# Row numbers for the sparse expert slots: one-hot matmuls on chip in place of scatters to memory

## The chip, the cores and the metric

One Trainium2 chip, one of its cores. The metric is the device time of one execution in microseconds (us). Engines: PE (TensorE), DVE (VectorE), ACT (ScalarE), POOL (GpSimd), SP (SyncE, which here only issues DMAs).

## The reference

Three layers follow one another: a decaying linear attention (2 batches, 8 heads, 768 positions, 64 wide), a sparse mixture of experts, and a dense one.

```python
def reference(**kwargs):
    ...
    attn_out = _attn_ref(**attn_kwargs)
    x = np.ascontiguousarray(attn_out.transpose(0, 2, 1, 3)).reshape(B * S, H * D)   # 1536 rows of 512
    x = _moe_ref(x=x, **moe_kwargs)
    return _moe2_ref(x=x, **moe2_kwargs)

def _moe_ref(x, modality_id, w_gate, modality_bias, w1, w2):
    logits = x @ w_gate + modality_bias[modality_id]
    e_idx = np.argmax(logits, axis=1)                 # one of 8 experts for each row
    ...
    for e in range(E):
        mask = e_idx == e
        h = np.maximum(x[mask] @ w1[e], 0.0)
        out[mask] = gate_w[mask, None] * (h @ w2[e])

def _moe2_ref(x, w_gate, w1, w2):
    logits = x @ w_gate
    P = np.exp(logits - logits.max())
    for _ in range(8):
        ...                                           # rows and columns of P scaled in turn
    for e in range(E):
        out += P[:, e:e + 1] * (np.maximum(x @ w1[e], 0.0) @ w2[e])
```

## The kernel before

**Attention and routing** (`attention_and_routing`, lines 360 to 561). The 1536 tokens are M = 12 blocks of C = 128. A loop over t (line 510) interleaves, in one written order for all engines, the scores of block t, the outputs of block t-1, the gate scores of block t-2 (`rows`), and, for pairs of blocks, `gates` (the expert of each token, a one-hot `oh`), `weighted` (the rows scaled and stored to the DRAM table `xs`, a DMA on ACT's queue) and `place`. `place` (lines 182 to 199) counts with bf16 matmuls how many earlier tokens went to the same expert: `posf` is N times the expert's number plus the token's rank in that expert, and `posi` the same as an integer.

**Lists of rows.** `scatter_id` (lines 201 to 205) writes, for one block, 128 row numbers of 4 bytes each into the DRAM table `treg` at the places `posi`, by an indirect DMA on POOL's queue. 12 such scatters stand in the loop; `treg` is cleared by one DMA at the start (line 407). Whoever wants the rows of a slot reads 384 consecutive numbers of `treg` back into `gidx` (`gather_ids`, line 340, from a start that POOL loads into a register), and then gathers the rows of `xs` with three indirect DMAs (`gather_rows`, line 344).

**Sparse experts.** Tokens of an expert are worked on in slots of 272. One slot is early: after 6 blocks `early_table` (line 212) picks the fullest expert, SP starts to load its weights, and at t = 11 its rows are gathered and transposed (`xprep`, line 352). `early_slot` (line 587) computes it right after the attention and prepares slot 0. Then come at least NREST = 5 further slots (`rest_slot`, `slot`, lines 627 to 658); in this run exactly 5, called slots 0 to 4 below. A slot has steps f = 0 to 8: at f the first matmul group of piece f (`mm1`, 12 matmuls of 272 columns, evicted as `hb` by ACT and DVE), the second one of piece f-2 (`second_of`), the splitting of the next weights into two parts on ACT and DVE (`conv1`, `conv2`, by `split`, lines 297 to 306), which SP reloads behind it. At f = 0 it issues the gather of the next slot's rows and the read of the row numbers of the slot after that; at f = 4 and 5 it transposes the gathered rows.

**Compact positions.** Slots leave their results in `x2T` in the order of experts. The dense layer works in that order, and needs for each compact position the token it belongs to (`tokmap`), to scatter the output rows (line 849). `compact_ranks`, `compact_starts` and `compact_positions` compute the position of each token in slot 1; 12 further scatters (`compact_scatters`, 6 in slot 1 and 6 in slot 2) write the token numbers to the DRAM table `tokd`, and one DMA reads it back (line 972).

**Dense experts.** From about 277 us to the end; the change leaves its code as it is but for that one DMA.

The order on every engine is the order in which the program is written (`tc.manual_schedule()`). An engine that waits holds up all that is written behind it on that engine. The lines that the change is about:

```python
            inst = G.indirect_dma_start(out=treg, out_offset=bass.IndirectOffsetOnAxis(ap=posi[:, m:m + 1], axis=0), in_=seqi[:, m:m + 1], in_offset=None).ins
...
            G.dma_start(out=gidx[z], in_=treg[ds(pos, 384)].rearrange("(z p) o -> p (z o)", p=128))
...
                inst = G.indirect_dma_start(out=tokd, out_offset=bass.IndirectOffsetOnAxis(ap=posi[:, m:m + 1], axis=0), in_=toki[:, m:m + 1], in_offset=None).ins
```

## Time and profile before

| | |
|---|---|
| median of 3 runs | 1321.52 us (1318.6 to 1322.06) |
| the profiled execution | 1313.04 us, of which 1311.4 us are the span from its first to its last instruction |
| busy in the span | PE 96%, DVE 51%, ACT 38%, POOL 35% |
| mean granted TensorE clock | 0.985 of full speed |
| DMA | 117.76 MB, 61735 packets, 8376 of them under 512 B |

The profile names each instruction by line, engine, operation and tiles (written <- read). "Idle before" is the time for which the engine did nothing just before an instruction; the name behind "<-" is what ended that wait. PEclk is the clock that TensorE was granted (1.00 is 2.4 GHz, 0.50 is 1.2 GHz), DMA the busy share of the core's 16 DMA engines.

### The profile page before, as it was taken

The page shows a single profiled execution, that of the slowest core. Times are in us where ns is not written, and L with a number is a line of the kernel's source. Part 1 is how long each engine was busy: PE and PEld are TensorE (multiplying, and loading weights), DVE is VectorE, ACT ScalarE, POOL GpSimd, SP SyncE. Part 2 cuts the span into 40 slices and gives each one's busy share as a digit, 9 for nine tenths or more (in the row PEclk, how much of TensorE's full clock was granted, in tenths as well). Part 3 has the DMA queues.
Part 4 walks back from the last instruction along what each step waited for, and adds up shares of the span by engine and source line. Part 5 has one row for each costly group of instructions (what it writes and reads, how often), then busy time and mean ns, then how long its engine had stood idle before and what let it go on. Part 6 is the DMA issues. An engine that isn't in the chain of part 4 may idle for free.

```text
span 1311.4 us, 19165 instructions
## 1 busy us (share of the span) xinstructions
PE 1254.2 (96%) x7164; PEld 1141.5 (87%) x7164; DVE 664.6 (51%) x1248; ACT 498.4 (38%) x996; POOL 457.8 (35%) x464
## 2 busy tenths in 40 slices
PE   5868998989999999999999999999999999999997
PEld 4758997988999999999998999999999999999996
DVE  5546655646454545445454546354535454545453
ACT  1225545531234334333434342233433343434341
POOL 3532152014433333333333336333333333333332
PEclk9989998989999999999999999999999999999999
DMA  8887697530022222222222222222222222222201
GB/s 289 142 192 154 195 151 192 184 115 1 18 72 73 73 64 65 64 73 63 67 65 73 66 88 91 62 81 65 65 70 68 65 64 65 73 65 75 71 25 48
DMA packets 61735, 117.76 MB, mean 90 GB/s; under 512 B 8376, under 2 KB 10048, under 8 KB 61632
## 3 DMA queue, kind: packets, MB, share of 16 engines
q1 hardware_dynamic: 55744, 105.67, 29.1%
q0 software_dynamic: 3408, 7.14, 2.0%
q10 hardware_dynamic: 2480, 3.64, 1.2%
q8 instruction: 58, 0.95, 0.3%
q14 instruction: 45, 0.37, 0.1%
HBM read 110.05 MB, written 6.37 MB: 89 GB/s over the span
## 4 chain that ended last, share of the span: by engine, by line
PE 77%; DVE 1%; POOL 0%; issue 0%; POOLq 0%
PE banks L868 13%; PE banks L867 13%; PE banks L866 13%; PE banks L831 12%; PE banks L832 12%; PE banks L833 12%; PE banks L704 0%; POOL out_dram L849 0%; PE banks L710 0%; PE banks L736 0%; DVE Pm L730 0%; DVE Pm L740 0%; DVE tab L728 0%; POOLq L1004 0%; DVE tab L738 0%
## 5 line engine op out<-in xcount | busy, mean ns | idle before, releaser
L820 POOL TENSOR_TENSOR w1r<-sraw,w1r 128x1024 fp32r<-128x1024 f32 x56 | 134.6, 2403 | 573.1 <-ACT w1r L819 573.1
L868 PE MATMUL banks<-w2r,hb 128*128 128x512 f32 x750 | 294.7, 393 | 0.0
L867 PE MATMUL banks<-w2r,hb 128*128 128x512 f32 x750 | 294.1, 392 | 0.0
L866 PE MATMUL banks<-w2r,hb 128*128 128x512 f32 x750 | 291.6, 389 | 0.0
L868 PEld LDWEIGHTS banks<-w2r,hb 128*128 128x128 f32 x750 | 140.7, 188 | 29.6
L836 ACT ACTIVATE hb<-snap 128x384 fp32r<-128x384 f32 x168 | 87.8, 522 | 200.4 <-DVE snap L953 120.1
L831 PE MATMUL banks<-x2T,w1r 128*128 128x384 f32 x464 | 159.1, 343 | 3.5 <-DVEq L683 3.5
L832 PE MATMUL banks<-x2T,w1r 128*128 128x384 f32 x464 | 158.8, 342 | 0.0
L867 PEld LDWEIGHTS banks<-w2r,hb 128*128 128x128 f32 x750 | 140.7, 188 | 19.3
L866 PEld LDWEIGHTS banks<-w2r,hb 128*128 128x128 f32 x750 | 140.8, 188 | 19.1
L833 PE MATMUL banks<-x2T,w1r 128*128 128x384 f32 x464 | 157.3, 339 | 0.0
L833 PE MATMUL banks<-xt,w1r 128*128 128x384 f32 x448 | 151.1, 337 | 0.0
L831 PE MATMUL banks<-xt,w1r 128*128 128x384 f32 x448 | 150.8, 337 | 0.0
L832 PE MATMUL banks<-xt,w1r 128*128 128x384 f32 x448 | 150.8, 337 | 0.0
L837 DVE SCALAR_TENSOR_TENSOR hb<-snap,hb 128x384 fp32r<-128x384 f32 x168 | 103.2, 614 | 66.4 <-ACT hb L836 66.4
L837 DVE SCALAR_TENSOR_TENSOR hb<-banks,hb 128x384 fp32r<-128x384 f32 x88 | 49.0, 557 | 164.2 <-ACT hb L836 164.2
L836 ACT ACTIVATE hb<-banks 128x384 fp32r<-128x384 f32 x88 | 43.3, 492 | 212.8 <-PE banks L833 205.2
L299 DVE TENSOR_TENSOR w2r<-stg,w2r 128x512 fp32r<-128x512 f32 x155 | 107.4, 695 | 12.0 <-ACT w2r L298 11.8
L298 ACT ACTIVATE w2r<-stg 128x512 fp32r<-128x512 f32 x155 | 96.3, 624 | 11.2 <-DMA stg<-in_w_dram 11.2
L831 PEld LDWEIGHTS banks<-x2T,w1r 128*128 128x128 f32 x464 | 87.9, 189 | 9.3 <-ACTq L683 3.7
L832 PEld LDWEIGHTS banks<-x2T,w1r 128*128 128x128 f32 x464 | 88.1, 190 | 5.6
L832 PEld LDWEIGHTS banks<-xt,w1r 128*128 128x128 f32 x448 | 84.1, 188 | 7.3
(215 smaller groups left out, 2114.7 us busy)
## 6 DMA issues: line engine op xcount, KB each, us to landing
stg<-in_w_dram SPq DMA_DIRECT2D x349, 256.0 KB, 2.7
pk<-in_pack_dram SPq DMA_DIRECT2D x24, 512.0 KB, 9.2
xs<-xr ACTq DMA_DIRECT2D x12, 256.0 KB, 8.1
xrow<-in_w_dram SPq DMA_DIRECT2D x3, 256.0 KB, 5.0
maskT<-powd SPq DMA_DIRECT2D x2, 256.0 KB, 5.4
xrow<-xs,gidx POOLq DMA_INDIRECT x21, 4.4
gtab<-in_gtab_dram ACTq DMA_DIRECT2D x1, 272.0 KB
lamq<-powd SPq DMA_DIRECT2D x2, 128.0 KB
```

The costliest lines, as they stand in the source:

```text
L298: A.activation(out=dst[:, 0], in_=src, func=AF.Copy)
L299: eng.tensor_tensor(out=dst[:, 1], in0=src, in1=dst[:, 0].bitcast(F32), op=ALU.subtract)
L820: G.tensor_tensor(out=ws[:, 1], in0=sraw, in1=ws[:, 0].bitcast(F32), op=ALU.subtract)
L831: T.matmul(out=b, lhsT=w(0, kk), rhs=x(0, kk), start=start and kk == 0, stop=False, skip_group_check=True)
L832: T.matmul(out=b, lhsT=w(0, kk), rhs=x(1, kk), start=False, stop=False, skip_group_check=True)
L833: T.matmul(out=b, lhsT=w(1, kk), rhs=x(0, kk), start=False, stop=stop and kk == kks - 1, skip_group_check=True)
L836: A.activation(out=h[:, 0], in_=src, func=AF.Relu)
L837: V.scalar_tensor_tensor(out=h[:, 1], in0=src, scalar=0.0, in1=h[:, 0].bitcast(F32), op0=ALU.max, op1=ALU.subtract)
L866: T.matmul(out=bank[mi], lhsT=h[:, 0, tok], rhs=w[:, 0], start=first, stop=False, skip_group_check=True)
L867: T.matmul(out=bank[mi], lhsT=h[:, 0, tok], rhs=w[:, 1], start=False, stop=False, skip_group_check=True)
L868: T.matmul(out=bank[mi], lhsT=h[:, 1, tok], rhs=w[:, 0], start=False, stop=last, skip_group_check=True)
```

## The change

No list goes through memory any more. For a slot that begins at position p0, `ids_block` (on DVE) takes `posf - p0` of all tokens, finds for each token in which of the slot's three blocks of 128 places it falls (a one-hot `o`), and reduces the position to its place within the block. `ids_place` (DVE) makes of that place a one-hot row of 128, `idp`, in bf16, for 12 blocks of tokens. `ids_out` sums on PE, over the 12 blocks of tokens, one-hot places (128 weights) times `idr` (the row number in two parts, 128 times the block and the rest, times `o`), adds the two parts on DVE and writes the integers straight to `gidx`. The same three steps with 12 blocks of places give `tokmap`. For the early slot they run over its 6 blocks of tokens.

So the two DRAM tables, their clearing, the 24 scatters, the 8 reads of `gidx`, the read of `tokmap`, POOL's register loads and the integer copies `posi` are gone. Moved: the early slot's row gather from t = 11 to t = 9, its first transposes before `rows(10)` and its last before `rows(11)`; the splitting of its first two w2 pieces ahead of the branch; the rest of its splits and of slot 0's loads to other steps f of `early_slot`; slot 0's transposes into the middle of step 8; the `compact_` steps from f = 0, 1, 3 of slot 1 to f = 4, 5, 6.

```diff
         def place_last():
             place(M - 2, True)
-            for a in range(M - 2, M):
-                scatter_id(a)
...
-        def gather_ids(z, pos):
-            G.dma_start(out=gidx[z], in_=treg[ds(pos, 384)].rearrange("(z p) o -> p (z o)", p=128))
+        def ids_block(src, start, nm, nb, hi):
+            t, n = idt[:, 0, 0:nm], idt[:, 1, 0:nm]
+            ge = idg[:, 0:nm * (nb + 1)].rearrange("p (m b) -> p m b", m=nm)
+            o = ido[:, 0:nm * nb].rearrange("p (m b) -> p m b", m=nm)
+            if start is None:
+                V.tensor_copy(out=t, in_=src)
+            else:
+                V.tensor_scalar(out=t, in0=src, scalar1=start, scalar2=None, op0=ALU.subtract)
+            V.tensor_tensor(out=ge, in0=bc(t, 2, [128, nm, nb + 1]), in1=bc(k("blk")[:, 0:nb + 1], 1, [128, nm, nb + 1]), op=ALU.is_ge)
+            V.tensor_tensor(out=o, in0=ge[:, :, 0:nb], in1=ge[:, :, 1:nb + 1], op=ALU.subtract)
+            V.tensor_reduce(out=n, in_=ge[:, :, 1:nb + 1], axis=AX.X, op=ALU.add)
+            V.scalar_tensor_tensor(out=t, in0=n, scalar=-float(C), in1=t, op0=ALU.mult, op1=ALU.add)
+            V.tensor_tensor(out=idr[:, 0:nm, 0:nb], in0=o, in1=bc(hi[:, 0:nm], 2, [128, nm, nb]), op=ALU.mult)
+            V.tensor_scalar(out=idr[:, 0:nm, nb:2 * nb], in0=o, scalar1=k("plo"), scalar2=None, op0=ALU.mult)
+
+        def ids_place(nm):
+            V.tensor_tensor(out=idp[:, 0:nm], in0=bc(k("iota"), 1, [128, nm, C]), in1=bc(idt[:, 0, 0:nm], 2, [128, nm, C]), op=ALU.is_equal)
+
+        def ids_out(dst, nm, nb, b):
+            b = b[:, 0:2 * nb]
+            for m in range(nm):
+                T.matmul(out=b, lhsT=idp[:, m], rhs=idr[:, m, 0:2 * nb], start=m == 0, stop=m == nm - 1)
+            V.tensor_reduce(out=idf[:, 0:nb], in_=b.rearrange("p (z q) -> p q z", z=2), axis=AX.X, op=ALU.add)
+            V.tensor_copy(out=dst, in_=idf[:, 0:nb])
...
-                    if t == M - 1:
-                        gather_ids(1, pa)
-                        gather_rows(1, (MEARLY + 1) * C)
-                        scatter_id(MEARLY + 1)
-                        scatter_id(MEARLY + 2)
+                    if t == M:
+                        xprep(1, (0, 1), [bank[0], bank[1]])
...
+                        ids_block(posf[:, 0:MEARLY + 1], epos, MEARLY + 1, 3, k("xhi"))
+                        ids_place(MEARLY + 1)
+                    if t == MEARLY + 4:
+                        ids_out(gidx[1], MEARLY + 1, 3, bank[3][:, 40:46])
+                        gather_rows(1, (MEARLY + 1) * C)
...
-                xprep(1, (0, 1), at)
+                xprep(1, (2, 3), [None, None, bank[3], bank[0]])
                 rows(M - 1)
                 gates(M - 2)
-                xprep(1, (2, 3), at)
                 place_last()
...
+                early_conv2(0)
+                early_conv2(1)
...
-                        slot_ids(nxt + 1)
+                    if f in (1, 2, 4):
+                        slot_ids(nxt + 1)[f // 2]()
...
-                rest_slot(s, {1: {0: (compact_ranks,), 1: (compact_starts,), 3: (compact_positions,)}, 2: {1: (lambda: compact_scatters(range(M // 2, M)),)}}.get(s, {}))
+                rest_slot(s, {1: {4: (compact_ranks,), 5: (compact_starts,), 6: (compact_positions,)}, 2: {5: (lambda: ids_block(cposf, None, M, M, k("thi")),), 6: (lambda: ids_place(M),), 8: (lambda: ids_out(tokmap, M, M, rot()),)}}.get(s, {}))
...
-            points[3].setdefault(3, []).append(lambda: G.dma_start(out=tokmap, in_=tokd.rearrange("(m p) o -> p (m o)", p=128)))
```

Three places of the order of instructions. POOL's queue from slot 1 into slot 2 before (`tokd` is the table of tokens, `xrow` the gathered rows of a slot):

```order
L344 DMA xrow_119<-xs,gidx_117 128x512 x2
L344 DMA xrow_119<-xs,gidx_117 16x512
L347 TENSOR_LOAD sposi
L347 ISA x2
L340 REGISTER_ALU
L340 DMA gidx_118<-treg 128x3x1
L279 MEMSET gap 1x1
L280 DMA tokd<-toki,posi 1536x1
```

The last two rows are followed by 5 more such pairs, the next slot's gather and 6 pairs again. POOL's queue over the same slots now:

```order
L362 DMA xrow_115<-xs,gidx_113 128x512 x2
L362 DMA xrow_115<-xs,gidx_113 16x512
L362 DMA xrow_114<-xs,gidx_112 128x512 x2
L362 DMA xrow_114<-xs,gidx_112 16x512
L362 DMA xrow_115<-xs,gidx_113 128x512 x2
L362 DMA xrow_115<-xs,gidx_113 16x512
```

Only the gathers of rows are left on it. DVE in the loop of the attention, at the end of t = 8 and the start of t = 9, now (`At` is the masked score, `tab` holds the early table):

```order
L215 TENSOR_TENSOR tab<-cst,tab 128x8
L335 TENSOR_SCALAR idt<-posf,tab 128x6
L336 TENSOR_TENSOR idg<-idt,cst 128x24
L337 TENSOR_TENSOR ido<-idg 128x18
L338 TENSOR_REDUCE idt<-idg 128x6
L339 SCALAR_TENSOR_TENSOR idt<-idt 128x6
L340 TENSOR_TENSOR idr<-ido,cst 128x6x3
L341 TENSOR_SCALAR idr<-ido,cst 128x6x3
L344 TENSOR_TENSOR idp<-cst,idt 128x768
L445 TENSOR_TENSOR At_135<-banks,maskT 128x512 x2
```

Before, the masked score stood right behind the early table; eight operations have come between. DVE in the early slot, steps 0 to 2, now, behind the 15 operations of `tables` (`hb` is the eviction of a first-layer piece, `w1r` and `w2l` are split weights):

```order
L335 TENSOR_SCALAR idt<-posf,tab 128x12
L336 TENSOR_TENSOR idg<-idt,cst 128x48
L337 TENSOR_TENSOR ido<-idg 128x36
L338 TENSOR_REDUCE idt<-idg 128x12
L339 SCALAR_TENSOR_TENSOR idt<-idt 128x12
L340 TENSOR_TENSOR idr<-ido,cst 128x12x3
L341 TENSOR_SCALAR idr<-ido,cst 128x12x3
L312 SCALAR_TENSOR_TENSOR hb_937<-banks,hb_937 128x272
L344 TENSOR_TENSOR idp<-cst,idt 128x1536
L281 TENSOR_TENSOR w1r<-stg_105,w1r 128x512
L312 SCALAR_TENSOR_TENSOR hb_938<-banks,hb_938 128x272
L281 TENSOR_TENSOR w2l<-xrow_114,w2l 128x512
```

Before, two splits of w1 and one of w2 stood between `tables` and the second eviction; the two ids steps are new there, and two of the splits stand later or earlier.

## Rows read from the trace of the kernel before

**Rows 1.** Busy time by stage: us, PE, PEld, DVE, ACT, POOL, PEclk, DMA share, GB/s.

```profile
62.00:79.00 17.00, 6.52 (x91) 5.68 (x91) 8.07 (x26) 2.19 (x6) 4.65 (x5) 0.83 0.99 221
...
99.60:132.50 32.90, 28.20 (x204) 27.07 (x204) 22.87 (x58) 17.82 (x40) 9.16 (x11) 0.95 0.76 163
...
186.20:220.80 34.60, 28.97 (x206) 27.46 (x205) 18.84 (x38) 16.80 (x38) 14.68 (x19) 0.90 0.88 171
220.80:247.20 26.40, 26.40 (x207) 25.62 (x206) 16.95 (x33) 14.67 (x32) 0.00 (x0) 1.00 0.56 177
...
273.70:1311.40 1037.70, 1024.95 (x5108) 925.86 (x5108) 501.57 (x835) 385.80 (x746) 373.97 (x353) 0.99 0.21 65
```

**Rows 2.** Waits of PE from 0 to 100 us: total, times, longest.

```profile
PE banks L479 <- ACT xT L463: 18.3, 5, 9.1
PE banks L431 <- DMA pk<-in_pack_dram: 5.8, 2, 4.4
```

**Rows 3.** Waits of PE from 99.6 to 274 us.

```profile
PE banks L324 <- DVE hb L330: 5.4, 2, 4.9
PE banks L577 <- DVE w2l L299: 2.7, 1, 2.7
PE banks L324 <- DVE xsl L358: 2.0, 1, 2.0
```

**Rows 4.** Timeline of ACT from 77 to 78 us: start, duration, instruction, idle before.

```profile
77.50 0.33 ACTq L504 DMA_DIRECT2D xs<-xr  x1
77.87 0.60 ACT L463 ACTIVATE xT<-banks 128x512 f32<-128x512 f32 x1 [6.99 <-DMA xs<-xr]
```

**Rows 5.** Timeline of PE at the same place.

```profile
78.52 2.18 PE L479 MATMUL banks<-gtab,xT 128*128 128x136 f32 x8 [9.13 <-ACT xT L463]
```

**Rows 6.** Three narrower stretches, columns as in the first group.

```profile
66.40:74.00 7.60, 2.98 (x56) 2.55 (x52) 4.90 (x13) 1.05 (x3) 2.47 (x3) 0.94 1.13 115
73.00:83.40 10.40, 4.88 (x35) 4.46 (x37) 1.01 (x7) 1.33 (x3) 0.59 (x1) 0.51 0.93 312
202.80:209.70 6.90, 3.88 (x17) 3.88 (x18) 4.15 (x9) 3.73 (x9) 0.00 (x0) 0.51 1.13 199
```

**Rows 7.** DMA issues of the page: count, KB each, median us from issue to landing.

```profile
treg<-seqi,posi POOLq DMA_INDIRECT x12, 12.2
tokd<-toki,posi POOLq DMA_INDIRECT x12, 10.9
```

**Rows 8.** Timeline of POOL, scatters: one at 60 us, first and last of the other table.

```profile
60.79 0.97 POOL L203 DMA_INDIRECT treg<-seqi,posi  x1 [0.21 <-issue]
...
171.58 1.26 POOL L280 DMA_INDIRECT tokd<-toki,posi  x1 [28.04 <-DVE posi L274]
...
196.55 0.97 POOL L280 DMA_INDIRECT tokd<-toki,posi  x1 [3.04 <-DMA xrow<-xs,gidx]
```

**Rows 9.** Timeline of SP's queue: the early expert's w1.

```profile
64.93 14.47 SPq L295 DMA_DIRECT2D stg<-in_w_dram  x8
```

**Rows 10.** DMA issues of weights in slot 2, 186.2 to 220.8 us.

```profile
stg<-in_w_dram SPq DMA_DIRECT2D x17, 256.0 KB, 11.2
```

**Rows 11.** The same in slot 3, 220.8 to 247.2 us.

```profile
stg<-in_w_dram SPq DMA_DIRECT2D x16, 256.0 KB, 4.3
```

**Rows 12.** Waits of ACT in slot 2, 186 to 221 us.

```profile
ACT w2r L298 <- DMA stg<-in_w_dram: 9.2, 3, 5.0
```

**Rows 13.** Timeline of PE at 45.7 us, two bf16 matmuls each with its own weights.

```profile
45.71 0.17 PE L185 MATMUL banks<-ohsum,onesb 128*128 128x16 bf16 x1
45.74 0.17 PE L186 MATMUL banks<-oh,trib 128*128 128x16 bf16 x1
```

**Rows 14.** DVE operations on small tables: duration ns min/median/max.

```profile
L727 DVE TENSOR_REDUCE tab<-Pm x8: 252/253/254, 299.8 to 331.7; 128x12 f32<-128x96 f32 x8
L728 DVE TENSOR_SCALAR tab<-tab x8: 173/174/690, 300.0 to 332.0; 128x12 f32<-128x12 f32 x8
```

**Rows 15.** A DVE group from 99.6 to 132.5 us: busy, mean ns, idle before.

```profile
L299 DVE TENSOR_TENSOR w1r<-stg,w1r 128x512 fp32r<-128x512 f32 x13 | 8.4, 686 | 2.0 <-ACT w1r L298 1.7
```

More of the change, by code (lines that the diff above doesn't have):

```diff
@@ L199, in place @@
                     V.tensor_tensor(out=ohsum, in0=ohsum, in1=oh[:, m + a], op=ALU.add)
-        def scatter_id(m):
-            G.memset(gap, 0.0)
-            inst = G.indirect_dma_start(out=treg, out_offset=bass.IndirectOffsetOnAxis(ap=posi[:, m:m + 1], axis=0), in_=seqi[:, m:m + 1], in_offset=None).ins
-            tc.declare_no_dep(inst, group="reg_scatter", reason="entries of different tokens are disjoint")
-            tc.add_to_no_dep_group("reg_scatter", inst)
         def place_last():
             place(M - 2, True)
-            for a in range(M - 2, M):
-                scatter_id(a)
         def early_table():
@@ L271, in compact_positions @@
             V.tensor_tensor(out=scr, in0=oh, in1=bc(sti, 1, csh), op=ALU.mult)
-            V.tensor_reduce(out=posf, in_=scr, axis=AX.X, op=ALU.add)
-            V.tensor_tensor(out=posf, in0=posf, in1=early, op=ALU.mult)
-            V.tensor_tensor(out=posi, in0=posf, in1=rank, op=ALU.add)
-            compact_scatters(range(M // 2))
-        def compact_scatters(ms):
-            for m in ms:
-                G.memset(gap, 0.0)
-                inst = G.indirect_dma_start(out=tokd, out_offset=bass.IndirectOffsetOnAxis(ap=posi[:, m:m + 1], axis=0), in_=toki[:, m:m + 1], in_offset=None).ins
-                tc.declare_no_dep(inst, group="tok_scatter", reason="entries of different tokens are disjoint")
-                tc.add_to_no_dep_group("tok_scatter", inst)
+            V.tensor_reduce(out=cposf, in_=scr, axis=AX.X, op=ALU.add)
+            V.tensor_tensor(out=cposf, in0=cposf, in1=early, op=ALU.mult)
+            V.tensor_tensor(out=cposf, in0=cposf, in1=rank, op=ALU.add)
         rot_n = [0]
@@ L342, in gather_rows, with slot_ids, all_ids @@
+        def slot_ids(s):
+            return ((lambda: ids_block(posf, sposf[:, s:s + 1], M, 3, k("xhi"))), (lambda: ids_place(M)), (lambda: ids_out(gidx[s % 2], M, 3, rot())))
+        def all_ids(s):
+            for fn in slot_ids(s):
+                fn()
         def gather_rows(z, lim):
@@ L405, in attention_and_routing @@
                 load(3, 1)
-                G.memset(zid, 0)
-                G.dma_start(out=treg.rearrange("(p m) o -> p (m o)", p=128), in_=zid)
                 V.memset(ones, 1.0)
@@ L568, in build, with second_of @@
             x2T = [xp.tile([128, 4, XPAD], F32R, name=f"x2T{u}") for u in range(2)]
-            def second_of(f, hs):
+            def second_of(f, hs, part=slice(0, 8)):
                 order = [(dc, f - 2) for dc in range(4)] if f < 8 else [(0, 6), (1, 6), (0, 7), (1, 7), (2, 6), (2, 7), (3, 6), (3, 7)]
-                for dc, ff in order:
+                for dc, ff in order[part]:
                     dcs = slice(dc * 128, dc * 128 + 128)
@@ L587, in early_slot @@
             def early_slot():
-                hs = []
+                hs, ids = [], slot_ids(0)
                 for f in range(9):
                     if f < 8:
-                        hs.append(mm1(f, lambda t, kk: xsl[1][:, t, kk], SLOT, bank[f] if f < 2 else None))
-                    if f >= 2:
+                        hs.append(mm1(f, lambda t, kk: xsl[1][:, t, kk], SLOT, (bank[2], bank[1])[f] if f < 2 else None))
+                    if f == 8:
+                        second_of(f, hs, slice(0, 4))
+                        xprep(0)
+                        second_of(f, hs, slice(4, 8))
+                    elif f >= 2:
                         second_of(f, hs)
@@ L622, in early_slot @@
                     conv1(u, e)
-                xprep(0)
                 for u in range(4):
```

85 lines of the change are left out of this document (43 added, 42 removed).

## The prediction

> **What bounds the kernel now.** I read the table of busy time by stage first [rows 1]. From 273.7 us on PE is busy for 1025 of 1038 us at granted clock 0.99: the dense layer is PE's alone and nothing there changes, except that one small read of `tokmap`, which nobody waits for, goes. So only the first 274 us can move. Slot 3 (220.8 to 247.2) shows what a sparse slot costs when nothing disturbs it: 26.4 us, all of it PE, clock 1.00, the DMA engines 0.56 busy. Slot 2 (186.2 to 220.8) issues the same matmuls (206 against 207 records) and takes 34.6 us, with PE idle for 5.6 us of it and clock 0.90. Before the slots, the stretch from 62 to 79 us has PE busy for 6.5 of 17 us, with the DMA engines at 0.99.
>
> Then the waits of PE. Up to 100 us its largest is for ACT's copy `xT`, 9.1 of 18.3 us in a single wait [rows 2]; `pk`, the packed q, k, v, costs 5.8 us in two waits, of which 4.4 is the very first load and 1.4 comes at 62 us. From 99.6 to 274 us it waits three times for longer than a microsecond [rows 3]: 4.9 us for an eviction `hb` (in slot 2), 2.7 for a split of w2 and 2.0 for the transposed rows `xsl` (both in the early slot).
>
> Then what stands behind the two long ones. The 9.13 us of PE [rows 5] are ACT's: ACT stood for 6.99 us in front of the issue of a store to `xs`, until an earlier store had landed, and the copy that PE wants is written behind that issue [rows 4]. In slot 2 ACT waits 9.2 us in three pieces for weights that have not landed, before splits of w2 [rows 12]; the next `hb` is behind one of them. Weights take 11.2 us from issue to landing there [rows 10], 4.3 us in slot 3 [rows 11]. In both places the DMA engines are taken but move little: from 66.4 to 74 us their share is 1.13 (queues overlap) at 115 GB/s, in slot 2 0.88 at 171, while slot 3 moves 177 GB/s with 0.56 [rows 1, 6]. What both stretches have in common is scatters of 4-byte entries in flight: they take 12.2 us (`treg`) and 10.9 us (`tokd`) from issue to landing [rows 7], and a pair of `treg` scatters had been issued by 61 us, the 12 `tokd` ones from 171.6 to 196.6 us [rows 8]. I read them as what clogs the engines, though the trace doesn't show a cause as such.
>
> **The change part by part.** The sum is made against the profiled execution, 1313.0 us, which is 8.5 us below the median of 1321.5.
>
> *The tokd scatters go* (12, with the read-back). Slot 2 should take what slot 3 takes: 26.4 - 34.6 = **-8.2 us**. This holds the 4.9 us wait, smaller ones, and a granted clock of 0.51 from 202.8 to 209.7 us, right behind the long wait [rows 6]. Bounds: -5.6 if only the idle time goes and not the clock, 0 if something else delays the weights.
>
> *The treg scatters, the clearing and the reads of gidx go* (12, 1 and 8 DMAs). In the attention the 6.99 us of ACT and the 1.4 us for `pk` go: -8.4. What is late next there is DVE: between the early table and the masked score stand eight new operations, and the gates of the next pair, on which ACT's `weighted` and so `xT` wait, are behind them on DVE. Seven are small; operations on 12 to 96 elements take 0.17 to 0.25 us [rows 14], so 7 x 0.2 = 1.4 us. The eighth makes 768 elements per partition; 512 take 0.69 us [rows 15], so 1.0 us. Together +2.4, all of it on that chain. Net **-6.0 us**. Bounds: from 73.0 to 83.4 us PE had 0.51 of its clock [rows 6]; with 4.9 us busy in that stretch, up to 2.4 us come back if the shorter wait leaves the clock up, and the 2.4 us on DVE could be covered: -10.8. At the other end the store's wait stays: about 0. I take the middle, since a wait of some 4 us is left for PE. The row gather that moves from t = 11 to t = 9 puts three issues on POOL ahead of `qd(10)`, which PE wants only at t = 11; nothing. The last four transposes of the early slot now wait, in bank 3, for DVE's `place`, the first ones fill a wait of PE: I set the two against each other at 0, 1 us either way.
>
> *The early slot.* DVE is busy for 22.9 of its 32.9 us [rows 1]. It gets two rounds of ids work: 2 x (7 x 0.2 + 3 x 0.69 + 2 x 0.17) = 7.6 us, just within the 10.0 us it is idle, so each new wait depends on the order. PE's 2.7 us for w2 go, as the first two w2 pieces are split before the branch, and the 2.0 us for `xsl`, as the transposes now lie inside step 8. Two waits replace them. The second eviction is behind `tables` (15 operations of that small kind, some 3 us) and the seven ids operations, and the second group of step 3 needs it: by walking both queues with these durations, 2.3 us. At the end DVE has to wait for PE's ids matmuls, then keeps, splits and only then evicts slot 0's first piece: 3.4 us, where before there was none. 5.7 - 4.7 = **+1.0 us**. Bounds: -4.7 (both old waits go, none comes) and +2.9 (all 7.6 us of DVE's work delay PE, less the 4.7).
>
> *The new matmuls.* 6 for the early gather, 2 x 12 in the early slot, 5 x 12 in slots 0 to 4, 12 for `tokmap`: 102 pairs of a weight load and a matmul of 6 or 24 columns. Two such bf16 pairs start 0.03 us apart in the trace [rows 13], so 12 take 0.4 us. Six groups stand in the slots, where PE is the bound: **+2.4 us**; the others lie in the stages above, whose waits hold them. A matmul itself lasts 0.17 us there, which is the upper end if the pairs did not overlap: 102 x 0.17 = 17.3 us. I take the spacing, as it is of the same kind (bf16, 128 x 128 weights, few columns). The Trainium skill speaks against it: its page "TensorE: Matmul & The Clock Gate" (Part 2: What happens when you issue a matmul) gives a weight load as the number of weight columns divided by 1.2, in ns, 107 for 128. By that an estimate for 102 pairs is 10.9 us, and the sum would come out some 8 us higher than mine; what that would be a case of is rival C.
>
> *DVE in the slots* gets 3.8 us for each, on 17.0 busy of 26.4; where an eviction is used two steps, some 6 us, after its matmuls; that cover lets me cost it at nothing. If that cover were gone it would be 3.8 us a slot. The moved `compact_` steps are the same operations.
>
> Sum: -8.2 - 6.0 + 1.0 + 2.4 = **-10.8 us**. 1302.2 for an execution like the profiled one, **1310.7 us** for the median.
>
> **The rivals.** A: only slot 2 gains. The stores at 70 us may be slow because SP asks for the early expert's weights from 64.9 us on, not because of scatters. For: those loads stand right there [rows 9]. Against: weights alone move fast (312 GB/s from 73.0 to 83.4 us), and 115 GB/s at full engines is not theirs [rows 6]. DVE's 2.4 us then hide in the wait: -8.2 + 1.0 + 2.4 = -4.8, 1316.7 us.
>
> B: the scatters are only late along with the rest, and the weights' own queue is what is slow in both places. Then nothing comes back and the additions stay: +1.0 + 2.4 = +3.4, 1324.9 us, not to be told from no change or just slower. For: the software queue's packets can be waiting as well as blocking. Against: slot 3 carries the same weights in 4.3 us. The Trainium skill's page "DMA: Bandwidth & Descriptors" (Bandwidth) lists 64 packets of a 4 KB transfer at 0.68 us of engine time; by that a scatter of 128 entries is an estimate of 1.4 us, too little to clog anything, which would make B the case.
>
> C, slower: the one-hot pairs do not overlap, as all 12 of a group add into the same columns of PSUM and each has new weights. Place: `ids_out` in each slot, on PE, the bound there. If a pair took two matmul durations, 0.34 us, 102 x 0.31 = +31.6 on my sum, 1342 us. It turns the sign beyond 0.3% from 0.03 + 14.8 / 102 = 0.175 us a pair. Against: the two pairs of the trace also add into the same columns with new weights each, at 0.03 us [rows 13].
>
> D: the clock of 73 to 83 us comes back too and DVE is covered in the attention: 4.8 us more, 1305.9 us.
>
> **How the numbers follow.** My forecast 0.65, A 0.17, B 0.08, C 0.04, D 0.06. The range, 1302 to 1318, holds the forecast with the bounds of its terms, A and D; B and C, 0.12, lie above it. About 0.3%, 4 us, is what a measurement can tell from no change. Faster: the forecast, D and three quarters of A, 0.84. Same: the rest of A and more than half of B, 0.09. Slower: C and the rest of B, 0.07.
>
> **What would show it.** Right: slot 2 as long as slots 1 and 3, to half a microsecond; weights landing there in 4 to 5 us; ACT no longer idle for 7 us in front of a store, and PE's wait for `xT` at t = 10 near 4 us; DMA share from 62 us to the early slot clearly below 0.99; new waits of PE for `hb` in step 3 of the early slot and at the start of slot 0; 12 ids pairs within 0.5 us. Wrong: slot 2 still above 30 us (B); ids pairs 0.15 us apart or more (C); an attention as long as before (A); or evictions that come late in every slot, which would mean that DVE's 3.8 us are not covered.

## The result, and the profile after

The changed kernel takes 1302.2 us, the median of 4 runs (1299.6 to 1303.0), beside 1321.8 us for the kernel before on the same chip (1318.6 to 1322.7): a ratio of 0.985, with a 95% interval of 0.983 to 0.987. The forecast was 1310.7 us, in a range of 1302 to 1318. The direction is right and the size too small: 11 us were forecast, 19.6 came. The time lies only 0.2 us inside the lower end of the range, and the same kernel in a second series (after_again below, 1301.8 us) lies just outside it, so that the range held by a hair.

The two profiled executions hide half of that. Before's took 1313.0 us, after's 1302.4, which differ by 10.6 us. Before's profiled execution was quick by 8.5 us against its other runs, while after's is like its others. So before was profiled a second time (run b_again below, 1321.2 us). The table takes each stage's length from the timeline of PE (first matmuls of `mm1` and of `second_of`; a slot goes from its first matmul to the next one's). The last column is the best kernel found, also below.

| stage, us | before | before, again | after | v2 |
|---|---|---|---|---|
| to the first matmul of the early slot | 99.6 | 100.2 | 89.4 | 90.4 |
| from there to slot 0's first second-layer matmul | 37.9 | 40.6 | 46.3 | 35.4 |
| from there to slot 1 | 22.4 | 21.8 | 22.2 | 23.7 |
| slot 1 | 26.4 | 26.4 | 26.5 | 26.6 |
| slot 2 | 34.6 | 39.0 | 26.8 | 26.8 |
| slots 3 and 4 | 52.9 | 52.9 | 53.3 | 53.3 |
| from the last second-layer matmul of the slots to the end | 1037.7 | 1038.6 | 1036.1 | 1036.5 |
| span | 1311.4 | 1319.5 | 1300.6 | 1292.6 |

The busy time by stage of the changed kernel, columns as in [rows 1]:

```profile
62.00:69.10 7.10, 4.66 (x76) 4.09 (x74) 5.49 (x25) 1.68 (x5) 0.62 (x2) 0.97 0.77 246
89.40:127.80 38.40, 31.32 (x228) 29.92 (x229) 27.11 (x75) 18.09 (x42) 3.50 (x3) 0.87 0.37 119
...
184.48:211.30 26.82, 26.82 (x230) 25.98 (x229) 20.28 (x46) 14.79 (x33) 2.85 (x3) 1.00 0.54 176
211.30:237.90 26.60, 26.60 (x223) 25.82 (x220) 21.44 (x49) 14.56 (x32) 2.75 (x3) 1.00 0.60 181
264.60:1300.60 1036.00, 1025.78 (x5108) 926.48 (x5108) 499.99 (x835) 385.80 (x746) 372.21 (x352) 0.99 0.20 65
```

Slot 2 is now a slot like slot 3: PE is busy all of it, at clock 1.00, and the DMA engines are at 0.54 where they were at 0.88. The early slot (89.4 to 127.8) is the stage that got worse: 7 us of idle PE and a clock of 0.87, while DVE is busy for 27 of its 38 us.

The waits of PE in the two halves, to set beside [rows 2] and [rows 3]:

```profile
PE banks L441 <- DVE At L445: 7.8, 1, 7.8
PE banks L489 <- ACT xT L473: 6.9, 4, 4.2
PE banks L441 <- DMA pk<-in_pack_dram: 4.6, 1, 4.6
PE banks L349 <- DVE St L481: 2.4, 1, 2.4
```

```profile
PE banks L584 <- DVE hb L312: 4.7, 1, 4.7
PE banks L306 <- ACT w1r L280: 2.2, 1, 2.2
PE banks L308 <- DVE w1r L281: 1.6, 1, 1.6
```

In the attention the 9.1 us for `xT` and the 1.4 us for `pk` are gone. (The 4.6 us are the first load's, as before. The 7.8 us for `At` come at the very start, where before had 6.7.) The new wait of 2.4 us (L349) is PE in front of the ids matmuls of the early gather, which write into a bank that DVE has first to read for `St`. Behind 89.4 us the three old waits are gone, and three new ones stand in the early slot and at the head of slot 0.

### The profile page after: what moved, and what is told of

Read it like the earlier page. It is cut to its first block, busy times and chain, and to the rows that moved or that the text cites. A ratio compares the mean times of both kernels' runs of the same rounds, so it can differ in the third digit from the quotient of the medians.

```text
span 1300.6 us, 19334 instructions
## 1 busy us (share of the span) xinstructions
PE 1256.5 (97%) x7266; PEld 1144.0 (88%) x7266; DVE 686.2 (53%) x1330; ACT 499.5 (38%) x996; POOL 421.2 (32%) x405
## 4 chain that ended last, share of the span: by engine, by line
PE 78%; DVE 1%; POOL 0%; issue 0%; POOLq 0%
PE banks L887 13%; PE banks L886 13%; PE banks L885 13%; PE banks L850 12%; PE banks L851 12%; PE banks L852 12%; PE banks L723 0%; POOL out_dram L868 0%; PE banks L729 0%; PE banks L755 0%; DVE Pm L749 0%; DVE Pm L759 0%; DVE tab L747 0%; POOLq L1022 0%; DVE tab L757 0%
## 5 line engine op out<-in xcount | busy, mean ns | idle before, releaser
L855 ACT ACTIVATE hb<-banks 128x384 fp32r<-128x384 f32 x88 | 43.3, 492 | 212.5 <-PE banks L852 204.9
```

The source lines that it names most:

```text
L855: A.activation(out=h[:, 0], in_=src, func=AF.Relu)
```

## The experiments

Each kernel was timed beside the kernel before in the same series, and the ratio is to that.

| run | median us | runs | ratio to before | interval |
|---|---|---|---|---|
| b_again (before) | 1322.0 | 10 | 0.999 | 0.996 to 1.002 |
| after_again (after) | 1301.8 | 6 | 0.985 | 0.983 to 0.988 |
| a_tok, 4-byte scatters in the slots | 1318.7 | 10 | 0.995 | 0.992 to 0.997 |
| a_tok64, 64 bytes | 1315.3 | 4 | 0.993 | 0.991 to 0.994 |
| a_tok512, 512 bytes | 1304.3 | 6 | 0.988 | 0.986 to 0.990 |
| a_tokdir, 4 bytes, plain transfers | 1313.7 | 4 | 0.991 | 0.990 to 0.993 |
| a_treg, 4-byte scatters in the attention | 1316.7 | 10 | 0.995 | 0.992 to 0.997 |
| a_treg512, 512 bytes | 1307.1 | 4 | 0.991 | 0.988 to 0.994 |
| a_late | 1297.9 | 4 | 0.980 | 0.974 to 0.986 |
| v1_tail | 1301.7 | 5 | 0.986 | 0.984 to 0.989 |
| v1 | 1296.1 | 5 | 0.982 | 0.979 to 0.984 |
| v2 | 1292.9 | 5 | 0.976 | 0.975 to 0.977 |

The series ran on four chips, on which the medians of before lie between 1318.6 and 1324.6 us. A cost against the changed kernel is therefore given twice below, as a difference of medians and, in brackets, by the ratios: the difference to the changed kernel's 0.985, times 1322 us.

**How much do executions differ?** Both kernels again, unchanged.

> The kernel before, unchanged, for a second profiled execution. The first one ran 8.5 us under the median of the kernel's other runs. Theory: the extra 8.5 us lie where the small writes to memory are on the path, so that this execution, if it takes 1319 to 1323 us, has a longer way to the first matmul of the early slot (over 101 us, was 99.6) or a longer slot 2 (over 36 us, was 34.6), and the dense stage stays at 1034 us within 1.5. Rival: the extra time is the clock's, and the dense stage is longer by 5 us or more with the slots as they were. Time against before: ratio 1.000 within 0.003.

> The changed kernel, unchanged, beside the three that follow. Theory: without small writes in flight its executions differ little, 1300 to 1304 us, the early slot (first matmul to the first second-layer matmul of slot 0) 45 to 47 us again and slots 1 to 4 at 26.4 to 26.9 us each. Rival: the spread of the kernel before is the chip's and not the writes'; then this one spreads by 8 us or more between its executions too.

The second execution of before took 1321.2 us, and slot 2 is where more than half of the extra time lies: 39.0 us, not 34.6. The early slot has 2.7 us more, the dense stage only 0.9. (In the attention the single long wait of ACT in front of a store is 3.1 us here, not 7.0, and still the first matmul of the early slot comes at 100.2 us.) The weights of that slot, with the DMA shares, in the second execution of before:

```profile
189.06:228.09 39.03, 29.60 (x207) 28.25 (x205) 17.77 (x36) 15.47 (x37) 14.29 (x19) 0.87 0.90 145
```

```profile
q1 hardware_dynamic: 2214, 4.02, 68.4%
q0 software_dynamic: 781, 1.59, 21.4%
...
stg<-in_w_dram SPq DMA_DIRECT2D x17, 256.0 KB, 13.6
```

The same 17 weights that landed after 11.2 us in the first execution [rows 10] landed after 13.6. Of the changed kernel, slots 1 to 4 repeat to a hundredth of a microsecond (26.50, 26.82, 26.59, 26.66 twice). Its six runs still spread by 7.0 us, nearer to the rival's 8 than I had thought. Between the two profiled executions what differs is the early part, such as slot 0 with 30.2 and 33.2 us. The two shortest of the six (1297.2 and 1299.1 us) ran at a mean granted clock of 0.990, the others at 0.986 to 0.987; no trace here shows in which stage. In its series, before's 11 runs spread by 10.4 us.

**The scatters in the slots, put back.** The changed kernel with 12 scatters whose target is never read, then with other sizes and another kind. The `compact_` steps stand at their old places again in all four, so a_tok512 is also the control for that move:

```diff
+            V.tensor_copy(out=posi, in_=cposf)
+            compact_scatters(range(M // 2))
+        def compact_scatters(ms):
+            for m in ms:
+                G.memset(gap, 0.0)
+                inst = G.indirect_dma_start(out=tokd, out_offset=bass.IndirectOffsetOnAxis(ap=posi[:, m:m + 1], axis=0), in_=posi[:, m:m + 1], in_offset=None).ins
...
-                rest_slot(s, {1: {4: (compact_ranks,), 5: (compact_starts,), 6: (compact_positions,)}, 2: {5: (lambda: ids_block(cposf, None, M, M, k("thi")),), 6: (lambda: ids_place(M),), 8: (lambda: ids_out(tokmap, M, M, rot()),)}}.get(s, {}))
+                rest_slot(s, {1: {0: (compact_ranks,), 1: (compact_starts,), 3: (compact_positions,)}, 2: {1: (lambda: compact_scatters(range(M // 2, M)),), 5: (lambda: ids_block(cposf, None, M, M, k("thi")),), 6: (lambda: ids_place(M),), 8: (lambda: ids_out(tokmap, M, M, rot()),)}}.get(s, {}))
```

> The changed kernel with the twelve 128-entry scatters of compact positions put back, six in slot 1 after the positions are made and six in slot 2, as before; what they write is never read, the row table still comes from the matmuls. Theory: the small writes hold up the weights' transfers, so slot 2 goes from 26.8 us back to 33 to 36, the weights of that slot land 9 us or more after their issue (4 to 5 without), and the whole takes 1309 to 1312 us. Rival (rival A or B of the prediction turned round: the gain of slot 2 came from something else, such as the removed read-back of the table or the order of the table's vector work): slot 2 stays under 28 us and the whole at 1302 within 2.

With rows of 128 (a_tok512) or 16 (a_tok64) numbers:

```diff
-        tokd = dram.tile([N, 1], I32, name="tokd")
+        tokd = dram.tile([N, 128], F32, name="tokd")
...
-                inst = G.indirect_dma_start(out=tokd, out_offset=bass.IndirectOffsetOnAxis(ap=posi[:, m:m + 1], axis=0), in_=posi[:, m:m + 1], in_offset=None).ins
+                inst = G.indirect_dma_start(out=tokd, out_offset=bass.IndirectOffsetOnAxis(ap=posi[:, m:m + 1], axis=0), in_=cst[:, 0:128], in_offset=None).ins
```

> The changed kernel with the twelve scatters of compact positions put back as in a_tok, but with entries of 512 bytes (a row of 128 numbers) in place of 4 bytes; never read. Theory: the trouble is the size of the entries; 128 times the bytes in as many descriptors then cost little, slot 2 takes 27 to 30 us and the whole 1302 to 1306. Rival: it is the number of descriptors or the indirect write itself; slot 2 then takes 35 to 44 us as in a_tok and the whole 1312 us or more.

> The scatters of a_tok once more with entries of 64 bytes. With 4 bytes an entry slot 2 took 43.7 us, with 512 bytes 26.9. Theory: what counts is that an entry is a small part of a larger unit of memory, so 64 bytes cost nearly as much as 4: slot 2 over 33 us, landing of the scatters over 8 us, the whole over 1309 us. Rival: only neighbours count, several entries of 4 bytes falling into one unit of 64 bytes or less; with an entry to each 64 bytes the cost is gone: slot 2 under 29 us, the whole 1302 to 1306.

The same number of 4-byte writes without an index:

```diff
-                inst = G.indirect_dma_start(out=tokd, out_offset=bass.IndirectOffsetOnAxis(ap=posi[:, m:m + 1], axis=0), in_=posi[:, m:m + 1], in_offset=None).ins
+                inst = G.dma_start(out=tokd[m * C:(m + 1) * C, :], in_=posi[:, m:m + 1]).ins
```

> The twelve writes of a_tok as plain transfers: 128 entries of 4 bytes each, to 128 neighbouring places fixed beforehand, in place of the scatters by index. Theory: small entries are slow however they are addressed; slot 2 over 33 us, the whole over 1309 us. Rival: the cost is the indexed scatter with its 4-byte entries far apart; then slot 2 takes under 29 us and the whole 1302 to 1306.

Slots 1 and 2 of the four, by busy time (a_tok, a_tok512, a_tok64, a_tokdir):

```profile
159.20:187.30 28.10, 26.96 (x218) 25.88 (x218) 19.32 (x53) 12.67 (x28) 11.86 (x17) 1.00 0.75 136
187.30:231.00 43.70, 32.40 (x230) 30.27 (x229) 22.82 (x51) 16.35 (x38) 8.79 (x12) 0.80 0.78 132
```

```profile
157.70:185.30 27.60, 26.67 (x218) 25.80 (x217) 21.98 (x58) 14.66 (x32) 12.09 (x18) 1.00 0.59 186
185.30:212.20 26.90, 26.90 (x230) 26.06 (x229) 20.33 (x46) 14.79 (x33) 8.11 (x12) 1.00 0.60 194
```

```profile
158.20:197.70 39.50, 31.69 (x218) 28.96 (x217) 22.39 (x58) 14.45 (x32) 16.08 (x26) 0.87 0.42 126
197.70:224.60 26.90, 26.90 (x230) 26.06 (x229) 20.04 (x46) 14.79 (x33) 2.84 (x3) 1.00 0.54 174
```

```profile
158.80:188.10 29.30, 27.30 (x219) 25.99 (x218) 20.10 (x54) 13.07 (x28) 8.74 (x23) 1.00 0.81 142
188.10:224.20 36.10, 29.65 (x230) 28.08 (x229) 22.06 (x50) 15.72 (x37) 4.04 (x6) 0.91 0.69 150
```

And the DMA queues over both slots, first of a_tok, then of a_tok512:

```profile
q1 hardware_dynamic: 4601, 8.38, 67.8%
q0 software_dynamic: 768, 1.12, 8.6%
...
stg<-in_w_dram SPq DMA_DIRECT2D x31, 256.0 KB, 5.8
tokd<-posi POOLq DMA_INDIRECT x12, 13.1
```

```profile
q1 hardware_dynamic: 4591, 8.36, 49.1%
q0 software_dynamic: 768, 1.90, 10.0%
...
stg<-in_w_dram SPq DMA_DIRECT2D x31, 256.0 KB, 3.3
tokd<-cst,posi POOLq DMA_INDIRECT x12, 2.6
```

And where ACT stands in slot 1 of a_tok64, and the queue of the weights there:

```profile
ACT hb L322 <- remote: 7.2, 1, 7.2
ACT hb L322 <- issue: 6.6, 2, 4.4
```

```profile
q1 hardware_dynamic: 4731, 8.61, 39.9%
...
stg<-in_w_dram SPq DMA_DIRECT2D x32, 256.0 KB, 3.6
```

Against the changed kernel's 1302 us, putting the 4-byte scatters back costs 16.7 us in the median (12.6 by the ratios), more than expected: the whole is at 1318.7, where 1312 was the upper end. The profiled execution is the longest of its ten (1321.9 us); slot 2 takes 43.7 us in it, where 36 was the most expected, and holds nearly all of the loss. With 128 times the bytes in as many entries the cost is 2.3 us (3.7), so the number of entries and the indexed write are not it.

The entries' own packets are cheap: the 12 scatters are 192 packets of 32 bytes, 13 ns each in the trace. What grows is the weights': 67.8% of 16 x 71.8 us over 4601 packets is 169 ns each, against 93 ns with 512 bytes (49.1% of 16 x 54.5 us over 4591). Most of them are as quick as ever, a median of 84 ns in both; but 5 in 100 take more than half a microsecond, up to 8.9, and these hold half of the time. Small writes slow some of the other queue's packets, and weights land late. Plain 4-byte transfers do it too (11.7 us, or 7.7; 145 ns a packet over both slots, where the changed kernel has 87), so the index is not needed for it.

Entries of 64 bytes cost 13.3 us (10.2), but not in the same way. The weights' packets take 39.9% of 16 x 68 us over 4731, 92 ns each, the weights land after 3.6 us, and slot 2 is undisturbed. The loss lies in slot 1, where from 181.5 to 193.1 us PE is busy for 4.7 of 11.6 us at a DMA share of 0.30, while ACT stands in the two waits shown, for which the profile names no work of this core. So neither theory nor rival came whole, and why there is open. From which size on an entry harms the other queue can't be told from these runs either. Nor do they part the size from the place: 1536 entries of 4 bytes lie side by side in a table of 6 KB, those of 512 bytes in one of 768 KB. A run with 4-byte entries 512 bytes apart would tell.

**The scatters in the attention, put back**, at their old places, with 4 and with 512 bytes an entry:

```diff
+        def scatter_id(m):
+            G.memset(gap, 0.0)
+            inst = G.indirect_dma_start(out=treg, out_offset=bass.IndirectOffsetOnAxis(ap=posi[:, m:m + 1], axis=0), in_=posi[:, m:m + 1], in_offset=None).ins
...
                         place(t - 4)
+                        if t - 4 != MEARLY + 1:
+                            scatter_id(t - 4)
+                            scatter_id(t - 3)
```

> The changed kernel with the twelve 128-entry scatters of positions of the attention stage put back at their old places, written to a table that is never read and not cleared; gidx still comes from the matmuls. Theory: the writes delay the stores of the rows and the loads of the packs behind them, so the first matmul of the early slot goes from 89.4 back to 96 us or later, and the whole takes 1308 us or more. Rival: the attention gained by what does not come back here, the clearing of the table, the read of gidx and the place of the first splits; then the first matmul stays under 91.5 us and the whole at 1302 to 1304.

> The attention's twelve scatters of a_treg with entries of 512 bytes in place of 4. With 4 bytes the first matmul of the early slot came at 97.9 us, without any at 89.4. Theory: the attention lost its time to the same thing as slot 2, writes of small entries; with 512 bytes the first matmul comes under 91.5 us, the packs land in half the 13.2 us, and the whole takes 1302 to 1306 us. Rival: in the attention it is the scatters' issue on the POOL queue, ahead of the key and query scaling, whatever the size; the first matmul then stays over 96 us and the whole over 1310.

The DMA issues from 20 to 98 us, of a_treg and of a_treg512:

```profile
q1 hardware_dynamic: 4115, 11.54, 66.9%
...
pk<-in_pack_dram SPq DMA_DIRECT2D x13, 512.0 KB, 13.2
xs<-xr ACTq DMA_DIRECT2D x10, 256.0 KB, 10.2
```

```profile
q1 hardware_dynamic: 4192, 11.83, 45.9%
...
pk<-in_pack_dram SPq DMA_DIRECT2D x13, 512.0 KB, 4.7
xs<-xr ACTq DMA_DIRECT2D x12, 256.0 KB, 2.9
```

The first matmul of the early slot comes at 97.9 us with 4 bytes, at 94.9 with 512 and at 89.4 without scatters. The landing times fall just as in the slots, and ACT's wait in front of a store to `xs`, 7.0 us before, is back with 4 bytes (5.2 us) and gone with 512: that cause is as forecast. But only 3.0 of the 8.5 us go with the size of the entries, and 5.4 stay, so theory and rival share it.

What stays begins at 47.6 us, where a scatter on POOL's queue has stood 1.9 us for DVE's positions. POOL's products for two blocks (`Sd`, `kd`, `qd`), which are written behind it, then come nearly in one run, from 49.9 to 55.9 us. The gates' small operations on DVE fall beside them, and some of these last until the product beside them ends; the eleven take 5.0 us (51.2 to 56.2), where the changed kernel takes 2.3 (51.7 to 54.0). The rows' weighting (`xr`) on ACT waits for them, and PE for `xT`. First a_treg512, then the changed kernel:

```profile
51.43 1.28 POOL L469 TENSOR_TENSOR qd<-pk,lamq 128x512 f32<-128x512 f32 x1
...
51.41 1.34 DVE L508 TENSOR_TENSOR sm<-sm,btok 128x16 f32<-128x16 f32 x1
...
54.86 1.10 DVE L517 TENSOR_SCALAR sm<-sm 128x2 f32<-128x2 f32 x1
...
56.20 0.84 ACT L524 ACTIVATE xr<-banks,sm 128x256 f32<-128x256 f32 x2 [2.62 <-DVE sm L518]
...
58.09 1.91 PE L500 MATMUL banks<-gtab,xT 128*128 128x136 f32 x8 [3.41 <-ACT xT L484]
```

```profile
54.01 0.84 ACT L513 ACTIVATE xr<-banks,sm 128x256 f32<-128x256 f32 x2 [0.97 <-DVE sm L507]
...
55.90 1.19 PE L489 MATMUL banks<-gtab,xT 128*128 128x136 f32 x8 [0.74 <-ACT xT L473]
```

PE is 2.2 us behind from there. The granted clock right behind that wait (0.57 from 58 to 62 us) makes it 3.8 us by 62.8 us, and the rest comes in later waits. This chain is read from the traces; no run here tests it by itself. By the medians the 4-byte scatters cost 14.7 us (12.3 by the ratios), the 512-byte ones 5.1 (7.4); a_treg's profiled execution (1310.0 us) was 6.8 us quicker than its median, so the trace shows too small a share for the size.

**The early slot's order.** First the tables and slot 0's block numbers moved behind the second eviction, and the placing matrix (`ids[1]`) one step later:

```diff
                     if f == 0:
+                        early_conv1(4, ea)
+                    elif f == 1:
                         tables()
                         ids[0]()
                         e = expert(0)
-                    elif f == 1:
+                    elif f == 2:
                         ids[1]()
-                        early_conv1(4, ea)
-                    elif f == 2:
                         early_conv2(2)
                         early_conv1(5, ea)
```

> The changed kernel with one piece of the early slot's order altered: the tables and the block numbers of slot 0's ids are worked out after the second hidden block is evicted, not between the first and the second, and the placing matrix one step later. Theory: the 4.7 us wait for the second eviction and the half clock behind it are what lengthened the early slot; it goes from 46.3 us (first matmul to the first second-layer matmul of slot 0) to 38 to 42, and the whole to 1294 to 1298 us. Rival: the early slot is set by when its splits of weights come, after the late stores on ScalarE; then the wait only changes its name and the slot keeps 45 us or more, the whole 1301 to 1303.

The 4.7 us are gone, and 2.4 us for the placing matrix and 0.7 us for an eviction stand in their place. The stage is 43.3 us, 1.3 above what was expected and not the rival's 45. The median of the whole fits, though the four runs (1294.4 to 1301.2 us) reach over the rival's times too. And 4.0 us of this profile's gain are not the early slot's: no half clock comes at the start of the dense stage here, whose stretch is 1032.1 us (1036.1 in the changed kernel).

Then the splits near the end of the branch moved behind it, between the first hidden blocks of slot 0:

```diff
                 keep(0)
-                for u in range(3, 7):
-                    conv1(u, e)
-                for u in range(4):
-                    conv2(u)
...
+                if nxt == 1:
+                    conv1(3, ec)
+                    for f in range(2):
+                        hs.append(mm1(f, lambda t, kk: xsl[z][:, t, kk], SLOT))
+                        conv1(4 + f, ec)
+                        conv2(f)
+                    conv1(6, ec)
+                    conv2(2)
+                    conv2(3)
```

> The changed kernel with the splits of slot 0's blocks 3 to 6 of the first layer and 0 to 3 of the second taken out of the branch of the early slot and put between the first two hidden blocks of slot 0. Theory: the two waits of 2.2 and 1.6 us at slot 0's first matmuls, which read block 0, are for the last split of the branch, because the code after the branch waits for all of it; they go, the first second-layer matmul of slot 0 comes 3 to 4 us sooner after the first matmul of the early slot, and the whole takes 1298 to 1299.5 us. Rival: VectorE has the same splits to do and slot 0 loses the time one or two blocks later; slot 0 to slot 1 grows by what its head gained, and the whole stays within 1 us of the changed kernel.

The waits for splits of the branch go, as theory had it, and it brings nothing: the stage is 42.2 us, 4.1 shorter; and the way from there to slot 1 is 26.0 us, 3.8 longer. The whole is at 1301.7, as the rival had it. v1 adds the early slot's order, and also moves the tables ahead and the two last stores of rows to SP:

```diff
                 place_last()
+                tables()
                 weighted(M - 2)
...
-                early_conv2(0)
-                early_conv2(1)
...
-                    A.dma_start(out=xs[m * C:(m + 1) * C, :], in_=xw)
+                    (SP if m >= M - 2 else A).dma_start(out=xs[m * C:(m + 1) * C, :], in_=xw)
...
                     if f == 0:
-                        tables()
-                        ids[0]()
+                        early_conv2(0)
                         e = expert(0)
                     elif f == 1:
-                        ids[1]()
+                        early_conv2(1)
                         early_conv1(4, ea)
+                        ids[0]()
                     elif f == 2:
                         early_conv2(2)
+                        ids[1]()
```

> The same, and besides: the tables are worked out right after the last positions, where VectorE idles 3.4 us; the stores of the last two row blocks are issued by the SP queue rather than by ScalarE; the splits of the second-layer blocks 0 and 1 and slot 0's block numbers come after the first and second evictions. Theory: the early slot's loss is order on VectorE and ScalarE; its PE waits of 4.7 us and over go, with the half clock behind them, first matmul to slot 0's first second-layer matmul falls from 46.3 to 36 to 39 us, and the whole to 1291 to 1295 us. Rival: VectorE is full there (the ids' vector work of 2.9 us a slot has no room at all), so the waits come back at later blocks: 42 us or more, and 1297 us or more.

The stage is 35.9 us, 10.5 less than in the changed kernel, with no wait over 0.7 us inside; the whole is 1 us above what was expected, and slot 0 still has its splits and the ids on DVE together. v2 takes the ids of slot 0 out of their way:

```diff
-                    if f in (1, 2, 4):
-                        slot_ids(nxt + 1)[f // 2]()
+                    if f in ((4, 6, 8) if nxt == 1 else (1, 2, 4)):
+                        slot_ids(nxt + 1)[f // 2 - 2 if nxt == 1 else f // 2]()
```

> v1 with the three steps of slot 2's ids moved in slot 0 from blocks 1, 2 and 4 to blocks 4, 6 and 8, where VectorE has no splits left over from the early slot. Theory: the PE waits of 0.8 and 1.1 us in slot 0 and the half clock of 3.4 us behind them go, slot 0 falls from 31.5 to 27.5 to 29 us and the whole from 1296 to 1292 to 1294 us. Rival: the waits move to the later blocks or to slot 1's first gather; slot 0 and slot 1 together stay within 0.7 us of v1's 58.0 us and the whole within 1 us of 1296.

The one wait of PE above 0.7 us from 90.4 to 160 us in v2:

```profile
PE banks L306 <- DVE hb L312: 1.6, 1, 1.6
```

1292.9 us, 2.4% below before and 9 us below the change (12 by the ratios). From the first matmul of the early slot to slot 1 it takes 59.0 us, where the changed kernel takes 68.6 and before took 60.3 and 62.5, though it does all of the ids' vector work. So that work had room. Several things moved together on the way from the changed kernel to v2 (splits, tables, ids, two stores), and these runs do not part their shares.

## Why the prediction was right, and where its terms were not

**The tokd scatters: right, mechanism shown.** -8.2 was forecast, -7.8 came against the profiled execution and -12.2 against the second one, which stands at before's median. The sum set the term against one execution and then carried it to the median: that was the weak step, as the cost that goes is itself what varies (34.6, 39.0 and, put back, 43.7 us for slot 2). Rival B (the scatters only late along with the rest) fell with a_tok. It leaned on the Trainium skill's page "DMA: Bandwidth & Descriptors" (Bandwidth), by which I estimated 1.4 us of engine time for a scatter. The trace agrees that the scatters' own packets are cheap, 13 ns each. What failed is what B drew from it, that they then harm nothing: packets of the other queue went from 93 to 169 ns, and a scatter took 13.1 us to land. That 4-byte entries do this is shown by a_tok and a_tokdir beside a_tok512; whether by their size or by lying side by side is open.

**The attention: too small, -6.0 against -10.2.** The 2.4 us came in size, in one wait (L349), but not on the way that was forecast. The eight ids operations took 2.0 us on DVE (62.1 to 64.1 us); this is the last of them:

```profile
63.14 0.95 DVE L344 TENSOR_TENSOR idp<-cst,idt 128x768 bf16<-128x768 f32 x1
```

So PE's operand `idp` was there more than 3 us before PE began, at 67.6 us. PE waited for `St`, which DVE reads from the same bank at 67.1 us, behind the ids operations, the masked scores and the gates. The chain that the prediction named (gates, `weighted`, `xT`) was as late, but lay beside that wait, and so the wait of some 4 us for `xT` did not come: behind 40 us the longest is 1.3. All waits for `xT` together fell from 18.3 to 6.9 us and those for `pk` from 5.8 to 4.6, where 7.0 and 1.4 were forecast. The 6.99 us of ACT for a landing was real; a_treg512 points to a second cause that the sum did not have, scatters that hold up POOL's products until they fall beside the gates on DVE. (The prediction took the small operations at 0.2 us each; in the same kernel they can take several times that beside POOL.) The stage came close to the upper bound of the term (-10.8), which is rival D's, but only in size: DVE was not covered, and the clock came back in part, with 3.4 us of PE's work at 0.50 from 68.6 to 72.0 us, where before had 4.9 us at 0.51. Rival A fell: it would have left the attention as it was.

**The early slot: mis-sized, +8.4 against +1.0** (+5.7 against the second execution of before). The places were right: a wait for the second eviction, and one at the head of slot 0. The sizes were 4.7 and 3.8 us, where the prediction had 2.3 and 3.4. The old waits of 4.7 us went. The timeline of DVE in the changed kernel shows the first error:

```profile
93.08 1.29 DVE L281 TENSOR_TENSOR w1r<-stg,w1r 128x512 fp32r<-128x512 f32 x2 [3.44 <-ACT w1r L280]
...
95.49 0.43 DVE L312 SCALAR_TENSOR_TENSOR hb<-banks,hb 128x272 fp32r<-128x272 f32 x1
95.84 0.20 DVE L218 TENSOR_TENSOR tab<-tab,cst 128x48 f32<-128x48 f32 x1
...
99.39 0.23 DVE L335 TENSOR_SCALAR idt<-posf,tab 128x12 f32<-128x12 f32 x1
...
100.57 0.43 DVE L312 SCALAR_TENSOR_TENSOR hb<-banks,hb 128x272 fp32r<-128x272 f32 x1
```

DVE idles for 3.4 us until ACT, busy with scaling and storing the last rows, comes to the splits. The first eviction is at 95.5, 6 us after the first matmul; then come all 22 operations of the tables and block numbers, and PE, which was there at 96.4, waits for them whole. I had priced the operations about right (some 4.4 us) and let them begin too early against PE. The second error is that the waits were given no price in clock. Behind each of the two the granted clock is at the lower of its levels, 1.2 GHz:

```profile
99.30:106.20 6.90, 5.14 (x23) 5.14 (x24) 5.39 (x14) 0.00 (x0) 0.00 (x0) 0.51 0.16 48
130.10:133.40 3.30, 3.30 (x16) 3.30 (x16) 2.87 (x5) 0.89 (x2) 2.00 (x2) 0.50 1.02 336
```

5.1 and 3.3 us of matmuls at half the clock are 2.6 and 1.7 us lost. 8.5 - 4.7 + 4.3 us, and 0.9 us for two groups of ids matmuls, make 9.0, near the 8.4. That the ids' 7.6 us fit into "the 10.0 us it is idle" was true, as v1 and v2 show; the bound of +2.9 took DVE's work alone into account and not the clock.

**The new matmuls: cheaper than forecast.** Slots 1, 3 and 4 are longer by 0.13 to 0.24 us, where 0.4 was taken. One group of 12 pairs in slot 0:

```profile
144.23 0.46 PE L349 MATMUL banks<-idr,idp 128*128 128x6 bf16 x12
```

12 pairs in 0.46 us, with the last one's 0.17 us in it, start 0.026 us apart. Rival C, at 0.34 us a pair, fell. The plain formula for a weight load on the Trainium skill's page "TensorE: Matmul & The Clock Gate" (Part 2) gives 107 ns; the trace does not agree here, and the prediction did not take up the faster load of 128 bf16 columns of which the same part tells.

**The rest.** DVE's work in slots 1 to 4 hides as forecast: PE is busy all of them. The dense stage is 1.6 us shorter, which no term had.

Against the profiled execution, the terms that were too pessimistic (attention -4.2, matmuls and slot 2 together -1.6, dense -1.6) and the one that was too optimistic (early slot +7.4) cancel, so that the spans differ by the 10.8 us that were forecast; that agreement is luck. The 19.6 us of the medians are the same account with slot 2 at its usual length: between the second execution of before and the changed kernel the spans differ by 18.9 us.

## What to carry to other kernels

Twelve small DMAs, each of 128 entries of 4 bytes, slowed the transfers beside them: where the DMA engines are taken and move little, look for entries of a few bytes in flight, and compute the index on chip or write whole rows. When such a cost is to go, profile the kernel twice, since a cost by contention differs from one execution to the next and a sum against one of them is off by that. Work that fits into an engine's idle time still has to be put where nobody queues behind it: with the ids operations in it, the early slot took 46.3 us in one order and 35 to 36 in others.

## What was not expected of the hardware

The size of the entries: 12 writes of 128 entries cost 16.7 us in all with 4 bytes an entry, 13.3 with 64 and 2.3 with 512 (12.6, 10.2 and 3.7 by the ratios). With 4 bytes, the packets that grow longer are those of the other queue, and of those a few; with 64 bytes they do not grow, and the loss is open.

Small DVE operations beside POOL's products: in a_treg512 an operation on 16 elements (L508, shown above) took 1.34 us while POOL scaled keys and queries, and ended within 0.04 us of the end of POOL's product; one on 2 elements with a single tile as input (L517) took 1.10 us and ended as near to the next product's end. The one on 16 elements took 0.49 us in the changed kernel, and others of the kind take 0.17.

The first matmuls after a branch: in the changed kernel they wait for splits near its end, though they read the first block, which was split long before. When those splits stood behind the branch (v1_tail), PE's first matmul came 0.4 us after the ids matmuls. What makes them wait was not tested.
